# Score tiles of two key tiles shared between VectorE and ScalarE, in a fused attention and gated MLP kernel

## The chip, the cores and the metric

The kernel runs on one core of one Trainium2 chip. Its engines are TensorE (PE; its weight loads are listed apart as PEld), VectorE (DVE), ScalarE (ACT), GpSimd (POOL) and SyncE (SP, which issues nearly all DMAs here). The metric is the device time of one execution in microseconds; lower is better. For a version that was run several times, the median counts.

## The reference

One layer norm feeds an attention of 32 heads and a gated MLP; both results are added to the input. All inputs and the output are bfloat16, with S = 2048 rows, D = 512 columns, heads of 16 columns and F = 1792.

```python
xn = layernorm(A_x)                                   # over the last axis, eps 1e-5
q, k, v = split_heads(xn @ A_wqkv)                    # 32 heads of 16
p = softmax(einsum("bhqd,bhkd->bhqk", q, k) * 16 ** -0.5)
attention = merge_heads(einsum("bhqk,bhkd->bhqd", p, v)) @ A_wo
gate, up = xn @ B_W_gate, xn @ B_W_up
mlp = ((gate * (gate > 0)) * up) @ B_W_down
return A_x + attention + mlp
```

`B_x` is an input that isn't used.

## The kernel before

**Tiling.** The queries are cut into 4 chunks of 512 (`c4`), the heads into 4 groups of 8 (`gg`), each group into its even and odd heads (`ee`), the keys into 16 tiles of 128 (`kt`). One (`c4`, `gg`, `ee`) is a block: 4 heads, 512 queries, 2048 keys. There are 32 blocks, and in each 16 key tiles: 512 combinations that the code calls keys.

For one key there are four score tiles `j` = 0 to 3, one for each head, of 128 keys x 512 queries. PE's array is split into two halves of 64 rows (`half`). A tile `j` uses half `j // 2`; which of the two heads whose columns lie in that half is meant is chosen by `p = j % 2` through the moving operand, a copy of the queries in which all other heads' rows are zero (`qT[..., 2 * p + ee, :]`). The stationary operand, the keys in `kT`, is therefore the same for `j` = 0 and 1, and the same for `j` = 2 and 3.

**Who takes the exponential.** ScalarE takes most keys. It works in units: a unit is one key and one `p`, two score tiles (`j` = `p` and `p + 2`) in two neighbouring PSUM banks, and one activation over 1024 columns turns both into probabilities in `ring` (L1654). There are 704 units; two sets of two banks alternate between them. VectorE takes 160 keys, the quads, all four tiles of each, by an approximation of the exponential in integer arithmetic (`quad`, L1607): one operation a tile from PSUM to `qd` (L1615), then two shifted copies of the four tiles at once, made mostly by POOL (L1629). How many quads a block has is in `QUADS`; where they lie follows from it and from `QUAD_SHIFT`.

**Weighted sums of the values** (PV). `pv_stream` (L1540) makes for each key one group of four matmuls in each half of the array, with the stationary tiles from `v_aug`; a quad has three such groups in each half, for the three patterns.

**Everything else** (projections of queries, keys and values, the MLP's three products, the output projection) is put between the attention's work as jobs. All matmuls of the main part are groups of four, 64 rows x 32 columns, with 512 moving rows, in one half of the array; the tiles that aren't ScalarE's share four PSUM banks (`P_b`), from which VectorE empties them.

**The order.** The program first builds a graph of 8,030 operations. A list written out in the file, `ORDER`, puts all of them in one sequence by their numbers, and each engine's queue is that sequence restricted to the engine. A second list, `SLOTS`, gives the buffer for each tile in turn. Waits on semaphores follow from the graph (`follow`, L543, and `emit`, L579).

**Weight loads.** Each matmul group has a load of its four stationary tiles, and a key that names them (`wkey`). `emit` walks PE's queue and leaves a load out when the half still holds tiles of the same name:

```python
            elif held[o.half] == o.wkey:
                o.load, o.wsrc = False, ()
```

The names are `("k", gg, kt)` for scores and `("v", gg, ee, kt)` for PV. Operations with another name, on the same half, between two of the same name, make a new load necessary.

Of the kernel before, what the change touches and what calls it, by code (L numbers as in the profile page):

```python
# [5 lines left out]
BF16 = mybir.dt.bfloat16  # L6
# [69 lines left out]
SC_ORDER = (0, 2, 1, 3)  # L76
# [11 lines left out]

ORDER = [
# [651 lines left out]
def bass_parallel_sum__mha_block__glu_gated_reglu__prompt_kernel(  # L741
# [13 lines left out]
    with ExitStack() as es:  # L755
# [379 lines left out]
        for bk in blocks:  # L1135
            for t in dve_kt[bk]:
                kinds[bk + (t,)] = KINDS[len(kinds) % len(KINDS)]
# [31 lines left out]
        def first(tile, w, t_w, bank, c, x, need, prio):  # L1169
            for dt in range(DT):  # L1170
# [7 lines left out]
                if dt:  # L1178
                    tile.w.append(o)
# [530 lines left out]
```

## Time and profile before

| | |
|---|---|
| Times of three runs | 677.11, 676.46, 674.73 us; median 676.46 us |
| The profiled execution | span 678.5 us from the first to the last instruction; it is one execution, taken apart from these three runs |
| Granted TensorE clock | 1.000 over the span |
| PE matmuls | 667.7 us busy, 22,348 instructions |
| PE weight loads | 394.5 us busy, 20,912 instructions |
| VectorE | 594.7 us busy, 1,001 instructions |
| ScalarE | 659.1 us busy, 721 instructions |
| GpSimd | 334.1 us busy, 345 instructions |
| DMA | 28.77 MB, 42 GB/s on average |

Busy time is the time in which at least one instruction of the engine was under way. Matmuls are pipelined, and so are ScalarE's activations: two may overlap, so that the pace of an engine is read from the starts of its instructions and not from their durations. A group's line gives the source line, the engine, what is written and read, the shape and the count; then the busy time and the mean duration of one; then the idle time of the engine ahead of it and what ended it. In the timeline a line gives the start and the length of a run of like instructions, with the idle time ahead of it in brackets.

### The profile page before, as it was taken

The numbers are of one execution on the slowest core, as the hardware profiler recorded it, in microseconds if no ns is written. First come the engines' busy times: TensorE is split into PE (matmuls) and PEld (weight loads), VectorE is DVE, ScalarE is ACT, GpSimd is POOL, SyncE is SP. The second block draws the span as 40 slices with busy tenths as digits, with TensorE's granted clock in tenths as the row PEclk, the third lists the DMA queues.
The fourth block names the chain that finished last, engine by engine and source line by source line (L and its number), as shares of the span: only waits on it lengthen the run. The fifth ranks groups of instructions, "written<-read, shape, count | busy, mean of one in ns | idle before, by whom it ended". The sixth has DMA issues, their size and how long they took to land.

```text
span 678.5 us, 46119 instructions
## 1 busy us (share of the span) xinstructions
PE 667.7 (98%) x22348; PEld 394.5 (58%) x20912; DVE 594.7 (88%) x1001; ACT 659.1 (97%) x721; POOL 334.1 (49%) x345
## 2 busy tenths in 40 slices
PE   8999999999999999999999999999999999999997
PEld 3455566565565766665665655555565555555663
DVE  8958999998998888999999787999999777889886
ACT  7999999999999999999999999999999999999995
POOL 3201554654546645555556535654546642535650
PEclk9999999999999999999999999999999999999999
DMA  6420111131411121110101110020200012020101
GB/s 195 58 71 13 43 32 27 24 95 40 118 38 28 37 57 29 27 54 19 38 7 26 36 42 22 23 74 4 59 7 19 22 44 72 23 80 15 31 4 43
DMA packets 51478, 28.77 MB, mean 42 GB/s; under 512 B 18840, under 2 KB 50328, under 8 KB 51288
## 3 DMA queue, kind: packets, MB, share of 16 engines
q1 hardware_dynamic: 51144, 25.70, 14.6%
q8 instruction: 169, 2.77, 1.7%
q14 instruction: 21, 0.17, 0.1%
q10 hardware_dynamic: 144, 0.13, 0.1%
HBM read 18.22 MB, written 2.10 MB: 30 GB/s over the span
## 4 chain that ended last, share of the span: by engine, by line
PE 95%; DVE 2%; ACT 1%; issue 1%; DMA 0%; SPq 0%; POOL 0%
PE ps L481 95%; ACT ring L1654 1%; DVE stats L945 0%; DMA x_sb<-in_A_x_dram 0%; DVE xn_sb L968 0%; SPq L858 0%; DVE xnT L1013 0%; DVE o_sb L1410 0%; DVE up_sb L1412 0%; DVE qf L1414 0%; ACT up_sb L937 0%; DVE o_sb L1407 0%; ACT up_sb L936 0%; POOL rstd L943 0%; ACT xn_sb L1429 0%
## 5 line engine op out<-in xcount | busy, mean ns | idle before, releaser
L1654 ACT ACTIVATE ring<-ps 128x1024 bf16<-128x1024 f32 x704 | 651.1, 1085 | 7.4 <-PE ps L481 6.5
L481 PE MATMUL ps<-qT,kT 64*32 64x512 bf16 x8192 | 470.5, 375 | 1.8 <-issue 0.7
L1615 DVE TENSOR_SCALAR qd<-ps 128x512 int16<-128x512 f32 x640 | 418.8, 685 | 53.4 <-PE ps L481 47.3
L1629 POOL INT64_ADD qd<-qd x312 | 321.0, 1043 | 282.0 <-PE ps L481 132.6
L481 PE MATMUL ps<-qd,v_aug 64*32 64x512 bf16 x3840 | 297.1, 375 | 0.5 <-issue 0.4
L1595 PEld LDWEIGHTS <-kT 64*32 64x32 bf16 x8156 | 178.9, 92 | 113.6 <-issue 26.6
L481 PE MATMUL ps<-ring,v_aug 64*32 64x512 bf16 x2816 | 241.6, 375 | 0.4 <-issue 0.2
L1567 PEld LDWEIGHTS <-v_aug 64*32 64x32 bf16 x5256 | 129.5, 92 | 61.2 <-issue 11.8
L481 PE MATMUL ps<-xnT,wgs 64*32 64x512 bf16 x1792 | 136.7, 375 | 0.6 <-issue 0.6
L481 PE MATMUL ps<-xnT,wus 64*32 64x512 bf16 x1792 | 135.9, 375 | 0.0
L481 PE MATMUL ps<-Wd,hT 64*32 64x512 bf16 x768 | 60.9, 375 | 0.0
L1048 PEld LDWEIGHTS <-wus 64*32 64x32 bf16 x1792 | 45.2, 92 | 22.4 <-issue 2.9
L1048 PEld LDWEIGHTS <-wgs 64*32 64x32 bf16 x1792 | 44.2, 92 | 22.4 <-issue 3.5
L1048 PEld LDWEIGHTS <-hT 64*32 64x32 bf16 x1792 | 44.5, 92 | 21.4 <-issue 2.7
L481 PE MATMUL ps<-Wv,hT 64*32 64x512 bf16 x512 | 44.2, 375 | 0.4 <-issue 0.4
L481 PE MATMUL ps<-Wk,hT 64*32 64x512 bf16 x512 | 43.8, 375 | 0.0
L1269 DVE SCALAR_TENSOR_TENSOR hT<-ps,up_sb 128x512 bf16<-128x512 f32 x56 | 38.5, 687 | 5.5 <-PE ps L481 4.8
L1265 DVE COPY up_sb<-ps 128x512 f32<-128x512 f32 x56 | 38.4, 686 | 3.0 <-PE ps L481 2.1
L481 PE MATMUL ps<-Wo_p,x_sb 64*32 64x512 bf16 x480 | 40.5, 375 | 0.1
L481 PE MATMUL ps<-xnT,Wq 64*32 64x512 bf16 x480 | 36.8, 375 | 0.0
L481 PE MATMUL ps<-xnT,Wk 64*32 64x512 bf16 x480 | 35.6, 375 | 0.9 <-DVE xnT L1013 0.8
L481 PE MATMUL ps<-Wv,xnT 64*32 64x512 bf16 x512 | 31.6, 375 | 0.5 <-DVE kT L1106 0.4
(81 smaller groups left out, 219.6 us busy)
## 6 DMA issues: line engine op xcount, KB each, us to landing
wus<-in_B_W_up_dram SPq DMA_DIRECT2D x38, 128.0 KB, 2.9
wgs<-in_B_W_gate_dram SPq DMA_DIRECT2D x38, 128.0 KB, 2.7
xr_sb<-in_A_x_dram SPq DMA_DIRECT2D x16, 128.0 KB, 2.3
qT<-qf SPq DMA_DIRECT2D x120, 16.0 KB, 2.6
o_sb<-o_sb SPq DMA_DIRECT2D x60, 32.0 KB, 2.4
out_dram<-xn_sb SPq DMA_DIRECT2D x15, 128.0 KB, 2.1
x_sb<-in_A_x_dram SPq DMA_DIRECT2D x8, 128.0 KB, 2.8
Wd<-in_B_W_down_dram SPq DMA_DIRECT2D x6, 128.0 KB, 2.8
```

Of the source, the lines that this page charges most:

```text
L481: return e.add_instruction(mybir.InstMatmult(name=e.bass.get_next_instruction_name(), engine=mybir.EngineType.PE, ins=[e.lower_ap(x), e.lo ...
L1048: e.ldweights(w()[rows, 32 * j:32 * j + 32], tile_position=(rows.start, 32 * j))
L1265: G.op("DVE", 603, lambda e: e.tensor_copy(up_sb[:, tup.slot, :], bank_of(tu)), reads=[tu], writes=[tup], prio=-590)
L1269: G.op("DVE", 603, lambda e: e.scalar_tensor_tensor(out=hT[:, th.slot, :], in0=bank_of(tg), scalar=0.0, in1=up_sb[:, tup.slot, :], op0=ALU ...
L1567: e.ldweights(vs(j), tile_position=(64 * half, 32 * j))
L1595: e.ldweights(ks(m), tile_position=(64 * half, 32 * m))
L1615: G.op("DVE", 601, lambda e, j=j, tx=tx: e.tensor_scalar(qd[:, tq.slot, 512 * j:512 * j + 512], ps[:, BANK[tx.slot], :], IBIAS[3], 0.0, op ...
L1629: G.op("POOL", POOL_NS, lambda e, x=x, n=n: e.int64_add(x().bitcast(I64), raw().bitcast(I64), SHIFTS[n + 1] * LANES), reads=[ti, tq, t_lib ...
L1654: exp_ops[u] = G.op("ACT", ACT_NS, lambda e, tr=tr, k0=k0: e.activation(ring[:, tr.slot, :, :], ps[:, 4 * k0:4 * k0 + 2, :], ACTF.Exp, sca ...
```

## The change

For every quad's key the list `MATES` names a second key tile of the same block, its mate, which belongs to ScalarE. The two exchange half of their tiles. VectorE's four score tiles are now `j` = 0 and 2 of its own key and `j` = 1 and 3 of the mate; ScalarE's two units of the mate are `j` = 0 and 2 of the mate and `j` = 1 and 3 of the quad's key. The quad's scores come in the order 1, 3, 0, 2: the mate's tiles first. The PV groups follow: a group's four stationary tiles are now two of one key tile and two of the other (`kts`), and it needs the values of both. The number of tiles, units, quads and groups on each engine stays what it was; `QUADS`, `QUAD_SHIFT` and the jobs are the same.

`emit` isn't changed: it leaves a load out wherever the half still holds the tiles of that name. `ORDER` and `SLOTS` are replaced as a whole; they hold the same 8,030 numbers and as many slots. A further line puts an ordering edge between the parts of the first projections.

```diff
-SC_ORDER = (0, 2, 1, 3)
+SC_ORDER = (1, 3, 0, 2)
...
+MATES = [[], [0, 8], [1, 3, 4, 6, 8], [1, 2, 4, 6, 9], [1, 2, 4, 6, 9, 12], ...]
...
 ORDER = [
...
 SLOTS = [int(c, 36) for c in (
...
+        mate = {}
+        for n, bk in enumerate(blocks):
+            for t, m in zip(sorted(dve_kt[bk]), MATES[n]):
+                mate[bk + (t,)], mate[bk + (m,)] = m, t
...
                 if dt:
+                    o.order.add(tile.w[-1])
                     tile.w.append(o)
...
-        def pv_stream(key, kt, src, reads, u, prio, src_eng=None):
-            key = part(key + (kt,))
+        def pv_stream(key, kts, src, reads, u, prio, src_eng=None):
+            key = part(key + (kts[0],))
...
-                    return v_flat[rows, kt, a:a + 32]
+                    return v_flat[rows, kts[j % 2], a:a + 32]
...
-                         load=vload, weights=[t_vones, t_v[kt]], wkey=("v", gg, ee, kt))
+                         load=vload, weights=[t_vones, t_v[kts[0]], t_v[kts[1]]], wkey=("v", gg, ee) + kts)
...
         def quad(key, u, prev):
+            other = key[:3] + (mate[key],)
...
             for j in SC_ORDER:
-                prev = score(key, j, tx, ...)
+                prev = score(other if j % 2 else key, j, tx, ...)
...
-                pv_stream(key[:3], key[3], ...)
+                pv_stream(key[:3], (key[3], mate[key]), ...)
...
             for sub in range(2):
-                prev_sc = score(key, p + 2 * sub, ts, ...)
+                prev_sc = score(key if not p else key[:3] + (mate.get(key, key[3]),), p + 2 * sub, ts, ...)
...
-                pv_stream(key[:3], key[3], ...)
+                pv_stream(key[:3], (key[3], mate.get(key, key[3])), ...)
```

More of the change, by code (lines that the diff above doesn't have):

```diff
@@ L87 @@
 QUADS = [0, 2, 5, 5, 6, 6, 4, 5, 6, 5, 5, 5, 6, 5, 5, 8, 5, 5, 4, 6, 6, 4, 6, 5, 5, 5, 5, 5, 5, 6, 5, 5]
+MATES = [[], [0, 8], [1, 3, 4, 6, 8], [1, 2, 4, 6, 9], [1, 2, 4, 6, 9, 12], [1, 2, 6, 9, 12, 15], [2, 5, 7, 12], [0, 2, 5, 6, 9], [1, 2, 3, 7, 10, 13], [0, 4, 8, 10, 12], [1, 2, 5, 6, 9], [1, 2, 4, 6, 8], [1, 2, 4, 6, 7, 12], [1, 3, 6, 8, 11], [1, 2, 4, 6, 9], [1, 3, 5, 7, 9, 13, 15, 11], [8, 10, 12, 14, 15], [5, 9, 11, 14, 15], [3, 6, 9, 11], [1, 2, 4, 7, 9, 14], [1, 2, 5, 9, 12, 15], [2, 5, 7, 10], [1, 2, 4, 6, 9, 12], [1, 4, 6, 9, 14], [1, 4, 6, 9, 11], [1, 2, 4, 5, 8], [1, 2, 4, 5, 8], [1, 2, 4, 5, 8], [0, 2, 4, 6, 10], [1, 2, 4, 7, 10, 14], [1, 2, 5, 9, 11], [1, 2, 3, 6, 11]]
@@ L427 @@
-    "934032106200317200212130290021e30f0421350020011200c0123401d00a1b420208012009617001123113103e11001f031203134130151010310c16d301431a1b01821291"
-    "026117210202112301e231f1021140015013401010001131c0032d14ab01830911376702130100110123")]
+    "000121133020010120122113230401510617000008193210a101b220c01330de1f3100110145203120210103a12b031013890617200c1d1001e30f1230016110741520003111"
+    "0a31b120811209c321d20e1f1130232130302167130011131830a01b21021453001cd230101899001613074120301231001a11ef0031100ab30120101001c23011d031030440"
@@ new lines @@
+    "1b3000516710020e1010f01331890002c321300103111240a2103210b601017200c301330dd01ef320134205800120320409021233e0210020401620173210a23311f203bc01"
+    "d304003145320008121020902101100301103670e11g022113f123201a113110b411513060134133207831101243009c11h1d30e21f320a320110b3014530002321331i40013"
+    "10103000167140300113890133j1ab1001ef1030c210321d1003101020331106730040114301052101200103189001001a1210bc2114120de131f00211123032001261020742"
+    "215020010111200a01210012031b1240211cd08121933030223131030111ef22011ab2410c201310d61731304003145220030512301811930013312302010212670c02163120"
@@ new lines @@
+    "0d11ef0001a014212002b01000020711893122041312010561137200211300120a1b40310020100181013019301ef300167300040013cd00331ab23100421024050011122002"
+    "103230821110209101ef200021cd00232410ab0206317200132102145100003010343001e01f3001233100c1331d0018930300124011ab301416701113022011124510220110"
+    "2203e1141f21101cd210189233001012230131ab300611322074015303021e02012f000218000922110311301011100041c110210d420102315002621700a011020b22112341"
+    "250381419300211011020c3210003d43013005603317012200e2114020f213ab00218012009c4301d2302013305001245132000121014001612130307c11d3300016a1b32023"
@@ new lines @@
+    "102e30f11189147302112310340123206501167080211013230c31241300de22113120f01a13109020b811193001012341000103141005631310c307c11d0010402101001a03"
+    "1b010d31ef0124101230010101673433040001503022011314891003110130c1213g10da0312300be3121f03082241113030719123h0312630742152000101200e322401020f"
+    "a201b212080121009c100d60312030743105031230030e001f3000231100413101a1301b0189231016017201400123c110d421510020131112000112220136212107a21041b1"
+    "201018920301ef20302112003310c300d6010213003703114204015320331ef11003301ab130803100130931230430010131201c011d0060123011210074315130101ef4320a"
@@ new lines @@
+    "102403112011b80192011023113403c311220d021140101e21001f02163171510341315020a3101b20008021130922313227031421450020101220cd031ef920a01230b60032"
+    "1307a1011204302042133120c0311200de111fb220143012530813219301a031b1024302313233061700023e0011120130e1110f102f11cd30401512032114893061111g3000"
+    "72312320331a232030b010h001e21f00021420114530i20132cd0832190206301207200j13012003e310003f02401032011014501210a1102130bc1d02210123101010204216"
+    "70230181020130129e10400fa232210002b310210131cd21034201305821934302331672023120203a1320b1cd3103e1f0014303100141011210520131111001318009c12101"
@@ new lines @@
+    "1000de24101f0011601207a32011b001000014015010108940c0120d6011230700143123230120a3320be231f203003110012145210140c31100d23311126702313231100a23"
+    "141020b01110230001891200112ef041153001203101cd1300123300430167010010112001a1511106013b01ef0332304131003571890030101cd3400001103120211a0380b2"
+    "113013021301360007e03139013f1400158330111309c11d32021132103311ab04113311670031311108120100942100205e2340120fc001d20200121ab00021110011e23241"
+    "0f23123033412350820193062311342020711012cd30201ab01061010200418902130014570001111023")]
@@ L1574, in pv @@
                     return ins
-                o = G.op("PE", 216, pv, reads=[t_vones, t_v[kt]] + reads, joins=[t], prio=prio, name="pv%d" % u, mode="half", half=half, bank=(t, 0), slack=PV_SLACK if src_eng is None else PAT_SLACK,
-                         load=vload, weights=[t_vones, t_v[kt]], wkey=("v", gg, ee, kt))
+                o = G.op("PE", 216, pv, reads=[t_vones, t_v[kts[0]], t_v[kts[1]]] + reads, joins=[t], prio=prio, name="pv%d" % u, mode="half", half=half, bank=(t, 0), slack=PV_SLACK if src_eng is None else PAT_SLACK,
+                         load=vload, weights=[t_vones, t_v[kts[0]], t_v[kts[1]]], wkey=("v", gg, ee) + kts)
                 pv_ops[key].append(o)
@@ L1613, in quad @@
                 tx = Tile("x", P_b, XBANKS)
-                prev = score(key, j, tx, lambda tx=tx: BANK[tx.slot], 0, u, u - 1000, [prev] if prev else [], 1, after=u - AHEAD)
+                prev = score(other if j % 2 else key, j, tx, lambda tx=tx: BANK[tx.slot], 0, u, u - 1000, [prev] if prev else [], 1, after=u - AHEAD)
                 G.op("DVE", 601, lambda e, j=j, tx=tx: e.tensor_scalar(
@@ L1634, in quad @@
             for t, x, more in ((ti, raw, [tq]), (ta, xa, []), (tb, xb, [])):
-                pv_stream(key[:3], key[3], [(lambda rows, j=j, x=x: x()[rows, 512 * j:512 * j + 512].bitcast(BF16)) for j in range(4)],
+                pv_stream(key[:3], (key[3], mate[key]), [(lambda rows, j=j, x=x: x()[rows, 512 * j:512 * j + 512].bitcast(BF16)) for j in range(4)],
                           [t] + more, u, u + PV_LAG, "DVE")
@@ L1651, in bass_parallel_sum__mha_block__glu_gated_reglu__prompt_kernel @@
             for sub in range(2):
-                prev_sc = score(key, p + 2 * sub, ts, lambda b=4 * k0 + sub: b, sub, u, u - 2000 + 0.1 * sub, [prev_sc] if prev_sc else [], 2, pair=u)
+                prev_sc = score(key if not p else key[:3] + (mate.get(key, key[3]),), p + 2 * sub, ts, lambda b=4 * k0 + sub: b, sub, u, u - 2000 + 0.1 * sub, [prev_sc] if prev_sc else [], 2, pair=u)
             tr = Tile("r%d" % u, P_ring)
@@ L1658, in bass_parallel_sum__mha_block__glu_gated_reglu__prompt_kernel @@
                 trs = [where[key + (i,)] for i in range(2)]
-                pv_stream(key[:3], key[3], [(lambda rows, j=j, trs=trs: ring[rows, trs[j % 2].slot, j // 2, :]) for j in range(4)], trs, u, u + PV_LAG)
+                pv_stream(key[:3], (key[3], mate.get(key, key[3])), [(lambda rows, j=j, trs=trs: ring[rows, trs[j % 2].slot, j // 2, :]) for j in range(4)], trs, u, u + PV_LAG)
             while made_q < len(quads) and (quads[made_q][0] <= u + AHEAD or u == NU - 1):
```

20 lines of the change are left out of this document (removed), and 630 rows, old and new, of the table ORDER.

## The prediction

> **What bounds the kernel now.** I read the page first: the busy times, then the costliest groups and the DMA queues.
>
> ```profile
> span 678.5 us, 46119 instructions
> PE 667.7 (98%) x22348; PEld 394.5 (58%) x20912; DVE 594.7 (88%) x1001; ACT 659.1 (97%) x721; POOL 334.1 (49%) x345
> PE 95%; DVE 2%; ACT 1%; issue 1%; DMA 0%; SPq 0%; POOL 0%
> L1654 ACT ACTIVATE ring<-ps 128x1024 bf16<-128x1024 f32 x704 | 651.1, 1085 | 7.4 <-PE ps L481 6.5
> L1615 DVE TENSOR_SCALAR qd<-ps 128x512 int16<-128x512 f32 x640 | 418.8, 685 | 53.4 <-PE ps L481 47.3
> L1595 PEld LDWEIGHTS <-kT 64*32 64x32 bf16 x8156 | 178.9, 92 | 113.6 <-issue 26.6
> L1567 PEld LDWEIGHTS <-v_aug 64*32 64x32 bf16 x5256 | 129.5, 92 | 61.2 <-issue 11.8
> q8 instruction: 169, 2.77, 1.7%
> ```
>
> PE and ACT both look full, and the chain of waits gives PE 95%. Two full engines can't both be the limit, so I went to the timeline of ScalarE alone, and looked at when its exponentials (L1654) start.
>
> ```profile
> 10.48 1.96 ACT L1654 ACTIVATE ring<-ps 128x1024 bf16<-128x1024 f32 x2
> ...
> 47.22 12.02 ACT L1654 ACTIVATE ring<-ps 128x1024 bf16<-128x1024 f32 x13
> ...
> 58.07 2.08 ACT L1654 ACTIVATE ring<-ps 128x1024 bf16<-128x1024 f32 x2
> ...
> 392.25 3.77 ACT L1654 ACTIVATE ring<-ps 128x1024 bf16<-128x1024 f32 x4 [0.17 <-PE ps L481]
> 396.67 7.49 ACT L1654 ACTIVATE ring<-ps 128x1024 bf16<-128x1024 f32 x8 [0.65 <-PE ps L481]
> ...
> 610.07 58.88 ACT L1654 ACTIVATE ring<-ps 128x1024 bf16<-128x1024 f32 x64 [0.29 <-PE ps L481]
> 669.43 0.66 ACT L1405 ACTIVATE up_sb<-ps 128x256 f32<-128x256 f32 x2 [0.48 <-PE ps L481]
> ```
>
> From 47.22 to 58.07 us twelve starts follow one another: 10.85 / 12 = 0.904 us from one exponential to the next, which is the pace of an undisturbed ScalarE (one takes 1.085, so they overlap). The 704 of them run from 10.48 to 610.07 + 58.88 = 668.95 us, 658.5 us. At the undisturbed pace they would take 703 x 0.904 + 1.08 = 636.6. So ScalarE is the limit, it does the same 704 exponentials after the change, and all that can be won between them is 658.5 - 636.6 = **22 us**. The page's idle time shows 7.4 of it; the rest is lateness that fits into the overlap of two exponentials and makes no gap.
>
> Each exponential waits for PE's scores. So the next question is why PE is late, and the timeline of PE around the larger gaps of ScalarE answers it.
>
> ```profile
> 394.98 0.38 PE L481 MATMUL ps<-Wd,hT 64*32 64x512 bf16 x4
> 395.10 0.38 PE L481 MATMUL ps<-qd,v_aug 64*32 64x512 bf16 x4
> 396.02 0.39 PE L481 MATMUL ps<-qT,kT 64*32 64x512 bf16 x4 [0.55 <-ACT ring L1654]
> 396.24 0.39 PE L481 MATMUL ps<-Wd,hT 64*32 64x512 bf16 x4
> 396.24 0.10 PEld L1048 LDWEIGHTS <-hT 64*32 64x32 bf16 x4
> 396.25 0.38 PE L481 MATMUL ps<-qT,kT 64*32 64x512 bf16 x4
> 396.45 0.39 PE L481 MATMUL ps<-Wd,hT 64*32 64x512 bf16 x4
> ...
> 562.50 2.85 ACT L1654 ACTIVATE ring<-ps 128x1024 bf16<-128x1024 f32 x3
> 564.65 0.38 PE L481 MATMUL ps<-Wv,hT 64*32 64x512 bf16 x2
> 565.40 0.38 PE L481 MATMUL ps<-Wv,hT 64*32 64x512 bf16 x2 [0.37 <-issue]
> 566.03 7.61 ACT L1654 ACTIVATE ring<-ps 128x1024 bf16<-128x1024 f32 x8 [0.68 <-PE ps L481]
> ...
> 591.25 2.88 ACT L1654 ACTIVATE ring<-ps 128x1024 bf16<-128x1024 f32 x3
> 592.57 0.38 PE L481 MATMUL ps<-xnT,wgs 64*32 64x512 bf16 x2
> 593.52 0.37 PE L481 MATMUL ps<-xnT,wgs 64*32 64x512 bf16 x2 [0.58 <-issue]
> 594.64 15.14 ACT L1654 ACTIVATE ring<-ps 128x1024 bf16<-128x1024 f32 x16 [0.51 <-PE ps L481]
> ```
>
> At 564.65 and at 592.57 PE stops in the middle of a group of four matmuls that share one wait: two start, then nothing for 0.75 and 0.95 us, then the other two. They need no new weights and no semaphore. What is missing is the instruction itself. Numbering PE's and PEld's records in order of start, I find 32 such stops (over 0.22 us without a start, and the next record carries no wait) between these two:
>
> ```profile
> 46.98 0.12 PEld L1048 LDWEIGHTS <-xnT 64*32 64x32 bf16 x11 [0.18 <-issue]
> ...
> 609.43 0.09 PEld L1567 LDWEIGHTS <-v_aug 64*32 64x32 bf16 x1 [0.57 <-issue]
> ```
>
> All 32 stand at a record number that leaves the same rest when divided by 256. The q8 row fits: 169 pieces for 22,348 + 20,912 = 43,260 PE instructions, 256 in each, and 2.77 MB / 43,260 = 64 bytes for one. Its share gives 0.017 x 16 x 678.5 / 169 = 1.1 us per piece. So **PE's instruction supply** runs dry at the seam of two pieces. The stops add up to 11.6 us (each counted beyond 0.06 us); 24 of them lie in 364 to 427 and 552 to 608 us.
>
> What a stop costs ScalarE: 392.25 + 4 x 0.904 = 395.87, and the next exponential came at 396.67, 0.80 late after a stop of 0.92 (395.10 to 396.02); by the same reckoning 0.82 late after 0.75 and 0.68 after 0.95. That is 2.30 for 2.62, 0.88. So the stops cost 11.6 x 0.88 = **10.2 us** of the 22.
>
> **The change part by part.** *Work that stays.* 704 exponentials, 640 evacuations on VectorE (L1615), the same matmuls, POOL additions and DMAs: VectorE's four tiles are only two heads each of two key tiles instead of four of one. Cost 0. Two dependencies are new: a quad needs keys and values of its mate too. For 91 of 160 quads the mate is the neighbouring key tile, and both lie in the same block; I price that at 0, with the keys' projection, due 32 units ahead, as its cover. Without the cover one quad would wait for at most a projection's place in the queue, and VectorE sits idle 53.4 us before these evacuations already.
>
> *Fewer weight loads.* A load is left out when the half of the array already holds that stationary tile. Counted in the order lists: before, 9 of 2,048 score groups and 350 of 1,664 PV groups go without, which gives (2048 - 9) x 4 = 8,156 and (1664 - 350) x 4 = 5,256 loads, just the counts of the two PEld rows. After, it is 355 and 618. That is 614 groups, 2,456 loads fewer, 5.7% of PE's instructions: 40,804, or 159 pieces.
>
> Price of the load itself: at 396.24 the next group's load (0.10) runs under a group that started at 396.24, and that half's next group starts at 396.45, 0.21 later, the time the moving rows take. A load so hidden gives back nothing: 0. What it gives back is room for the fetch. At ScalarE's pace, 256 instructions are 256 / (43,260 / 704) x 0.904 = 3.77 us of PE's work before and 256 / (40,804 / 704) x 0.904 = 3.99 us after. Each piece so gets 0.22 us more; taking 0.23 off every one of the 32 stops leaves 4.5 of 11.6 us. Gain 7.1 x 0.88 = **-6.2 us**. The ends: 0, if the loads are left out elsewhere than where the supply is short, and -10.2, if no stop is left, which neighbouring pieces make possible since relief is handed on.
>
> [...]
>
> *Order and score order (1, 3, 0, 2).* All queues are reordered, SP's and POOL's too; the first exponentials and the tail wait for the same work, 0. What I can read off the lists is how evenly PE serves ScalarE. Between the score pair of one unit and the next, the fuller half holds 4 groups in 440 gaps before, 5 in 203, 6 or more in 3; after, 4 in 247, 5 in 306, 6 in 57, 7 or more in 8. Over two gaps in a row 10 or more stand in 6 places before and in 98 after (88 with 10, 9 with 11, one with 12). A group takes 0.215 us (396.02 to 396.24 to 396.45). Two exponentials take 1.81. A score group can't start before the exponential two units back has ended (1.085), and its result starts the next 0.42 later (396.25 to 396.67), so 1.81 - 1.085 - 0.42 = 0.30 us is to spare. Ten groups, 2.15, are 0.04 over 1.81 + 0.30, eleven 0.255, twelve 0.47: 88 x 0.04 + 9 x 0.255 + 0.47 = 6.3 us, against 0.9 before. One heavy gap belongs to two such pairs, so I take half: **+2.7 us**. The ends: 0, and +25.6 when nothing is to spare (57 x 0.385 + 7 x 0.60 + 0.81 less 1.4 before).
>
> The remaining lateness, 22 - 10.2 = 11.8 us, comes from waits for banks and for VectorE, whose order is new as well. Nothing quoted says which way it moves: 0, with ends of half of it, -6 and +6.
>
> Sum: -6.2 + 2.7 = -3.5 us. Against the profiled execution (678.5 us, 2.0 above the median of the runs) that is 675.0; carried to the median of 676.46, **673.0 us**. About 0.3%, 2 us, is what a measurement of this kernel can tell from no change.
>
> **The rivals.** *All stops go and the order is better too.* For it: the supply is short by 0.36 us a stop on average, little more than a piece gains. Against it: the gaps counted above. -10.2, with up to half of the other 11.8: 660 to 668 us. 0.10.
>
> *The two effects cancel.* The relief is spread evenly, not where the 24 stops are, and the gaps cost the full 5.4: within 2 us of 676.5. 0.16.
>
> *The bunched order starves ScalarE: slower.* The place is the score pair behind six or more groups of its half. With half of the 0.30 already used up, as after any other wait, 57 x 0.235 + 7 x 0.45 + 0.66 = 17 us, less 0.9 before, +16 against -6.2: 686 us. It decides as soon as these 65 gaps cost more than 0.1 us each. For it: 65 against 3 is much, and 53.4 us of VectorE's waiting shows how little PE has in reserve. Against it: a light gap behind a heavy one pays some back. 0.27.
>
> *The saved instructions are worth nothing.* The stops stay, because a piece's own latency of 1.1 us and more sets them, not the number of instructions. Then 676.5 + 2.7 = 679.2 us. Against it: the common rest by 256. 0.05. [...]
>
> **How the numbers follow.** The forecast, 668 to 674.4, has 0.42. Faster by over 0.3%: 0.42 + 0.10 = 0.52; the same: 0.16; slower: 0.27 + 0.05 = 0.32. The range goes from 664, half of the best rival, to 686, the price of the bunched order; about one in ten lies on either side.
>
> **What would show it.** Right: PEld with about 18,456 instructions (kT 6,772, v_aug 4,184), q8 with 159 or 160 pieces, stops at seams few and below 5 us in sum, ScalarE's exponentials still 0.904 apart at best and their whole run 3 to 4 us shorter. Wrong: ScalarE's idle time before L1654 above 7.4 us with PE as releaser and no seam near; or as many seam stops as before with fewer instructions between them; or a VectorE that waits for PE much longer than 47.3 us, with the loss in the waits that I set at 0.

## The result, and the profile after

The changed kernel takes 711.55 us (median of 4 runs, 710.4 to 712.4) against 676.79 us for the kernel before on the same chip: 1.0507 times as long, 95% interval 1.0481 to 1.0532. It is **slower by 35 us**; the prediction had said 673.0, with 686 as its upper end. The profiled execution took 712.4 us.

The page of the kernel after, in the lines that answer to those of before:

```profile
span 710.6 us, 43731 instructions
PE 693.5 (98%) x22348; PEld 353.6 (50%) x18456; DVE 597.4 (84%) x1001; ACT 673.2 (95%) x721; POOL 335.6 (47%) x345
q8 instruction: 160, 2.62, 1.6%
PE 86%; DVE 4%; SPq 4%; DMA 2%; issue 2%; ACT 1%; POOL 1%; DVEq 0%; POOLq 0%
L1663 ACT ACTIVATE ring<-ps 128x1024 bf16<-128x1024 f32 x704 | 665.2, 1031 | 20.3 <-PE ps L484 15.0
L1624 DVE TENSOR_SCALAR qd<-ps 128x512 int16<-128x512 f32 x640 | 418.1, 685 | 62.9 <-PE ps L484 56.0
L1603 PEld LDWEIGHTS <-kT 64*32 64x32 bf16 x6772 | 146.0, 92 | 123.7 <-issue 37.2
L1575 PEld LDWEIGHTS <-v_aug 64*32 64x32 bf16 x4184 | 100.4, 92 | 74.7 <-issue 26.7
```

The loads are what the lists said: 6,772 and 4,184, 18,456 in all. VectorE's operations and their durations are the same. What grew is ScalarE's idle time ahead of its exponentials (L1663; 7.4 before, 20.3 now), with PE as releaser, and VectorE's wait for PE (47.3 before, 56.0 now). Both engines get their scores later. The timeline of ScalarE alone, its first and its last row of exponentials:

```profile
15.73 5.78 ACT L1663 ACTIVATE ring<-ps 128x1024 bf16<-128x1024 f32 x6 [0.71 <-PE ps L484]
...
663.38 37.18 ACT L1663 ACTIVATE ring<-ps 128x1024 bf16<-128x1024 f32 x39 [0.20 <-PE ps L484]
```

The 704 exponentials run from 15.73 to 663.38 + 37.18 = 700.56 us, 684.8 us; before it was 658.5, from 10.48 on. So 26.4 us are lost between exponentials and 5.2 ahead of the first, 31.6 of the 35 us; most of the rest is that the profiled execution of the kernel before was a long one (its span of 678.5 us lies above its median time of 676.5, and in the other runs the span is about 2 us shorter than the time). In what follows the **lateness** of a kernel is the sum, over its exponentials, of what the time from one start to the next exceeds 0.9045 us, ScalarE's own pace: 21.5 us before, 47.9 after.

Numbered as in the prediction (PE's sequencer records, 128 before, have to be counted too), PE's records now show **no stop** at a seam of its instruction pieces: 32 with 11.6 us before, 0 after. Whether the saved loads took them away or the slower pace did, a run below decides; in either case a much larger loss lies on top.

### The profile page after: what moved, and what is told of

Its sections match the earlier page's. It is cut to its first block, busy times and chain, and to the rows that moved or that the text cites. A ratio compares the mean times of both kernels' runs of the same rounds, so it can differ in the third digit from the quotient of the medians.

```text
span 710.6 us, 43731 instructions
## 1 busy us (share of the span) xinstructions
PE 693.5 (98%) x22348; PEld 353.6 (50%) x18456; DVE 597.4 (84%) x1001; ACT 673.2 (95%) x721; POOL 335.6 (47%) x345
## 4 chain that ended last, share of the span: by engine, by line
PE 86%; DVE 4%; SPq 4%; DMA 2%; issue 2%; ACT 1%; POOL 1%; DVEq 0%; POOLq 0%
PE ps L484 85%; DVE qd L1624 2%; ACT ring L1663 1%; SPq L1099 1%; DMA Wq<-in_A_wqkv_dram 1%; SPq L1260 1%; DMA o_sb<-o_sb 1%; SPq L1518 1%; PE ps L1181 0%; SPq L861 0%; POOL qd L1638 0%; SPq L1527 0%; DVE stats L948 0%; DVE hT L1277 0%; DMA rb<-rrec 0%
## 5 line engine op out<-in xcount | busy, mean ns | idle before, releaser
L1663 ACT ACTIVATE ring<-ps 128x1024 bf16<-128x1024 f32 x704 | 665.2, 1031 | 20.3 <-PE ps L484 15.0
L484 PE MATMUL ps<-qT,kT 64*32 64x512 bf16 x8192 | 486.2, 375 | 4.4 <-DVE qd L1624 2.4
L484 PE MATMUL ps<-qd,v_aug 64*32 64x512 bf16 x3840 | 262.5, 375 | 0.1
L484 PE MATMUL ps<-ring,v_aug 64*32 64x512 bf16 x2816 | 231.7, 375 | 0.6 <-DVE qd L1624 0.2
L1603 PEld LDWEIGHTS <-kT 64*32 64x32 bf16 x6772 | 146.0, 92 | 123.7 <-issue 37.2
L1575 PEld LDWEIGHTS <-v_aug 64*32 64x32 bf16 x4184 | 100.4, 92 | 74.7 <-issue 26.7
L484 PE MATMUL ps<-xnT,wgs 64*32 64x512 bf16 x1792 | 134.6, 375 | 0.4 <-PE ps L484 0.2
L484 PE MATMUL ps<-Wd,hT 64*32 64x512 bf16 x768 | 64.6, 375 | 0.1
L1051 PEld LDWEIGHTS <-wus 64*32 64x32 bf16 x1792 | 43.1, 91 | 35.5 <-issue 10.9
L484 PE MATMUL ps<-Wk,hT 64*32 64x512 bf16 x512 | 45.8, 375 | 0.0
```

The source lines that it names most:

```text
L484: return e.add_instruction(mybir.InstMatmult(name=e.bass.get_next_instruction_name(), engine=mybir.EngineType.PE, ins=[e.lower_ap(x), e.lo ...
L1051: e.ldweights(w()[rows, 32 * j:32 * j + 32], tile_position=(rows.start, 32 * j))
L1575: e.ldweights(vs(j), tile_position=(64 * half, 32 * j))
L1603: e.ldweights(ks(m), tile_position=(64 * half, 32 * m))
L1663: exp_ops[u] = G.op("ACT", ACT_NS, lambda e, tr=tr, k0=k0: e.activation(ring[:, tr.slot, :, :], ps[:, 4 * k0:4 * k0 + 2, :], ACTF.Exp, sca ...
```

## The experiments

The file has two separable parts: the new tiles (`MATES` and what follows from it) and the new `ORDER`, `SLOTS` and `SC_ORDER`. All ratios are to the kernel before, timed beside each kernel on the same chip; since the kernel before took 676.8 to 680.8 us on them, kernels timed on different chips are compared by ratio. Lateness and first exponential are read from one profiled execution of each kernel, which can lie a few us off its median: that of before lies about 3.5 us above, that of mates_old_order 2.2 below. Line numbers move where the list has more lines (L1663 becomes L1683).

| Kernel | Median us | Ratio, 95% interval | Lateness us | First exponential us |
|---|---|---|---|---|
| before | 676.79 | 1 | 21.5 | 10.48 |
| after | 711.55 | 1.0507 [1.0481, 1.0532] | 47.9 | 15.73 |
| mates_old_order | 676.58 | 0.999 [0.9963, 1.0017] | 15.8 | 10.29 |
| new_order_no_mates | 709.28 | 1.0491 [1.0469, 1.0513] | 45.9 | 14.77 |
| after_all_loads | 713.07 | 1.0543 [1.0524, 1.0563] | 48.6 | 15.02 |
| before_all_loads | 691.62 | 1.0191 [1.0142, 1.024] | 37.1 | 10.24 |
| after_first_loads | 708.15 | 1.0447 [1.0418, 1.0475] | 49.0 | 10.70 |
| after_interleaved | 695.73 | 1.0271 [1.0237, 1.0306] | 30.3 | 15.62 |
| before_uninterleaved | 710.55 | 1.0486 [1.0456, 1.0515] | 51.5 | 10.24 |
| after_interleaved_2 | 693.72 | 1.0183 [1.0133, 1.0233] | 32.6 | 12.52 |
| after_waits_later | 690.99 | 1.019 [1.0149, 1.0232] | 30.2 | 10.62 |
| after_alternated | 693.47 | 1.022 [1.0185, 1.0255] | 33.1 | 10.49 |
| after_evened | 688.75 | 1.0103 [1.0069, 1.0137] | 26.9 | 10.53 |
| mates_evened | 688.21 | 1.0154 [1.0127, 1.018] | 29.9 | 10.32 |
| mates_even_pess | 686.09 | 1.008 [1.0054, 1.0106] | 26.5 | 10.38 |
| mates_even_cal | 681.30 | 1.0015 [0.9982, 1.0048] | 23.2 | 10.33 |
| mates_waits_pe | 680.91 | 1.0033 [1.0005, 1.0061] | 20.9 | 10.52 |
| mates_waits_all | 682.94 | 1.0078 [1.0053, 1.0103] | 24.8 | 10.25 |
| mates_alternated | 680.63 | 1.0013 [0.9986, 1.0041] | 21.7 | 10.31 |
| mates_alternated_2 | 680.51 | 1.002 [0.9992, 1.0048] | 18.2 | 10.26 |

**The two parts apart.** mates_old_order has the new tiles in the old order, new_order_no_mates the old tiles in the new order:

```diff
 # mates_old_order: after, with before's lists
-SC_ORDER = (1, 3, 0, 2)
+SC_ORDER = (0, 2, 1, 3)
 ORDER = [
...
 # new_order_no_mates: before, with after's lists
-SC_ORDER = (0, 2, 1, 3)
+SC_ORDER = (1, 3, 0, 2)
 ORDER = [
...
```

> The tiles are shared between quad and mate as after the change, but all queues stand in the order of before, with the quad's scores in the old order 0, 2, 1, 3 (71 score groups and 350 PV groups go without a load, against 9 and 350). Theory order: the new order alone costs the time, and sharing tiles is free; 676 us, between 672 and 680, exponentials' idle time as before (7.4 us), first exponential near 10.5 us. Theory mates: sharing is what delays (PV groups need two key tiles, quads need the mate's keys); 695 to 712 us.

> The new order of all queues and the new score order 1, 3, 0, 2, with four tiles of one key tile for VectorE as before (62 score groups and 618 PV groups without a load). Theory order: 705 to 715 us, first exponential near 15.7 us, 35 to 50 us of lateness of the exponentials. Theory mates: 676 to 685 us.

Sharing the tiles costs nothing (0.999) and the new order alone costs nearly all (1.0491 of 1.0507). The quad's score order went with the lists in both kernels; it wasn't tried by itself. The old order with the new tiles, on its page:

```profile
L1663 ACT ACTIVATE ring<-ps 128x1024 bf16<-128x1024 f32 x704 | 649.3, 1093 | 3.4 <-PE ps L484 2.9
L1624 DVE TENSOR_SCALAR qd<-ps 128x512 int16<-128x512 f32 x640 | 418.5, 685 | 47.9 <-PE ps L484 41.9
q8 instruction: 168, 2.75, 1.8%
```

**The price of the loads.** Both kernels with every load made:

```diff
-            elif held[o.half] == o.wkey:
+            elif False:
```

> The changed kernel with every stationary tile loaded again, 973 groups or 3,892 loads more. Theory order: the queues' order sets the time, loads are hidden, and PE is slow enough that 256 instructions last 3.9 us: 711 to 717 us with few seam stops. Rival, loads left out do harm (a group without its own load is bound to the one before it): 690 to 705 us. Rival, the instruction supply is what the change lives on: seam stops come back as before, 10 us and more, 720 to 725 us.

> The kernel before with every stationary tile loaded again, 359 groups or 1,436 loads more; order and tiles unchanged. Theory supply: 44,696 PE instructions, a piece of 256 lasts 3.65 us instead of 3.77, so every seam stop grows by 0.12 us and more seams stop: 15 to 25 us of stops instead of 11.6, 680 to 689 us. Rival, the supply is worth nothing to the time: 675 to 678 us.

In the old order 1,436 loads more make it 1.0191 times as long; at 691.62 us, 690 by the ratio, it is above the theory's 680 to 689, so a load costs more there than was reckoned. The page shows where:

```profile
q8 instruction: 175, 2.87, 1.7%
L1654 ACT ACTIVATE ring<-ps 128x1024 bf16<-128x1024 f32 x704 | 656.6, 1057 | 17.4 <-PE ps L481 15.5
```

Its trace has 64 stops at the seams with 28.8 us, 17.2 more than before, and 15.7 us more lateness, 0.91 us for each us of stops (the profiled execution took 696.1 us, 4.5 above the median, so these two numbers are somewhat large). So instruction supply does limit the old order, and the price of 0.88 fits. In the new order 3,892 loads more change 1.0507 to 1.0543, with 8 stops and 2.3 us: there the loads are worth little either way, and nearly all stops are gone even with every load made. The reading that fits both, the author's own and not measured by itself: in the new order PE, late for other reasons, gives the supply the time that it needs for the next 256 instructions (28.8 us of stops in the old order and 2.3 in the new, with every load made in both). **The loads saved and the order's loss don't add up; the loss swallows the gain.**

**The head.** In the kernel after, the first query tile waits, as the timeline of its first microseconds shows:

```profile
11.92 1.90 PE L1181 MATMUL ps<-xnT,Wq 128*32 128x384 bf16 x32 [3.83 <-DMA Wq<-in_A_wqkv_dram]
...
13.45 1.57 ACT L1207 ACTIVATE qT<-ps,hmask 128x384 bf16<-128x384 f32 x4 [4.72 <-PE ps L1181]
```

The view of the tile Wq gives when its first DMA was issued, and how long its two DMAs took to land, in the kernel after and (second fence) before:

```profile
L874 SPq DMA_DIRECT2D Wq<-in_A_wqkv_dram x1: 516/516/516, 5.1 to 5.1; - x1
DMA to landing us min/median/max: 6.1/6.4/6.8
```

```profile
L871 SPq DMA_DIRECT2D Wq<-in_A_wqkv_dram x1: 434/434/434, 2.6 to 2.6; - x1
DMA to landing us min/median/max: 2.6/5.4/8.1
```

The first DMA is the one with 6.8 us in the kernel after and with 2.6 before: it was issued 2.5 us later, just behind two transfers of 512 KB (Wv at 4.09 and hT at 4.57 us; before, only four of 128 KB stood ahead of it), and took 4.1 us longer to land.

after_first_loads puts SyncE's first 16 DMAs back in the program's order; nothing else is moved:

```diff
 # SyncE's queue, first 16 entries of ORDER (23 is the first part of Wq)
-19, 20, 21, 22, 25, 24, 26, 29, 32, 23, 27, 33, 28, 30, 34, 31
+19, 20, 21, 22, 23, 24, 25, 26, 27, 28, 29, 30, 31, 32, 33, 34
```

> The kernel after with one edit: the first 16 DMAs of SyncE's queue (x, Wq, Wk, Wv) are issued in the order of the program, so the first part of Wq is fifth again instead of tenth. Theory: the first query tile waited 4.7 us for TensorE, which waited 3.8 us for this DMA; the first exponential starts at 11 to 12 us instead of 15.7 and the time falls by 4 to 5 us, to 706.5 to 708 us, with the lateness of the later exponentials as after (46 to 49 us). Rival (the head's later start is made by the order of TensorE's first groups, or is caught up later): 710 to 712.5 us.

```profile
10.70 5.69 ACT L1683 ACTIVATE ring<-ps 128x1024 bf16<-128x1024 f32 x6
```

The first exponential starts 5.0 us earlier and the time falls by 3.4 us (by the ratios 0.0060, 4.1 us), somewhat less than the 4 to 5 expected. The rest of the lateness is where it was: 49.0.

**How the halves stand in PE's queue.** In the new order groups of one half stand in longer rows: 176 rows of four or more against 34. after_interleaved moves groups only past groups of the other half; before_uninterleaved does the opposite to the old order. In both, each half's own sequence and its loads, and the queues of ScalarE, VectorE, GpSimd and SyncE, are unchanged. The edit to `ORDER` is of the kind (h0, h1: the halves):

```diff
 # PE's queue around unit 346, after (-) and after_alternated (+)
-score 346 h0, MLP h0, MLP h0, MLP h0, score 346 h1
+score 346 h0, PV h1, MLP h0, score 346 h1, MLP h0, quad score h1, MLP h0
```

> The kernel after with one edit: in TensorE's queue, groups of one half are moved ahead of or behind groups of the other half (by at most a dozen entries at a time). Each half keeps its own sequence of groups and so its loads (973 groups without loads, as after), and the queues of ScalarE, VectorE, GpSimd and SyncE stay as they are. Theory (completions in queue order): a score pair is signalled only when the older groups of the other half are done, and a wait holds back everything queued behind it on both halves; taking out the places where a score pair stands behind a long run of the other half takes off 12 to 18 us: 693 to 700 us, the lateness of the exponentials falls from 47.9 to 30-36 us, and pairs signalled over 0.52 us after their last start fall from 72 of 704 to under 40. Rival (bunching within each half: too many groups fall into one gap between exponentials; or banks that are held too long): the sequences of the halves and of all other engines are unchanged, so 709 to 713 us.

> The kernel before with one edit: groups of TensorE's queue are moved at random by at most a dozen entries past groups of the other half only, until runs of four or more groups of one half are 120 (34 before, 176 after). Each half's sequence, the loads and all other queues stay as before. Theory (completions in queue order and waits that hold both halves): slower by 10 to 28 us, 687 to 705 us. Rival (the new order's loss comes from what falls into a gap on each half, or from banks): 674 to 679 us.

Both went the way of the theory: 15.8 us gained, and 33 us lost, 5 more than the top of that range, by nothing but the order of the two halves against each other. One figure missed: the pairs signalled over 0.52 us after their last start fell from 72 to 50 only, where under 40 were expected.

**What the order of the halves does** is seen at unit 346. The timeline of PE in the kernel after, then that of ScalarE:

```profile
352.11 0.58 PE L484 MATMUL ps<-qT,kT 64*32 64x512 bf16 x8
352.32 0.38 PE L484 MATMUL ps<-xnT,wgs 64*32 64x512 bf16 x4
352.52 0.38 PE L484 MATMUL ps<-qT,kT 64*32 64x512 bf16 x4
352.54 0.38 PE L484 MATMUL ps<-xnT,wgs 64*32 64x512 bf16 x4
352.74 0.38 PE L484 MATMUL ps<-ring,v_aug 64*32 64x512 bf16 x4
352.75 0.38 PE L484 MATMUL ps<-xnT,wgs 64*32 64x512 bf16 x4
```

```profile
349.10 3.83 ACT L1663 ACTIVATE ring<-ps 128x1024 bf16<-128x1024 f32 x4 [0.16 <-PE ps L484]
353.22 1.94 ACT L1663 ACTIVATE ring<-ps 128x1024 bf16<-128x1024 f32 x2 [0.29 <-PE ps L484]
```

The row at 352.11 holds two groups: unit 346 on half 0, and at 352.31 its other group on half 1. The three MLP groups on half 0 (`wgs`) stand between them in the queue, and all three start after the second score group. Yet the exponential starts at 353.22: 0.91 after that group, but 0.47 after the last of the three older MLP groups (352.75). It was due 0.9045 after the fourth of the row at 349.10 (351.91), at 352.81, so 0.41 are lost. In after_alternated the same groups start at the same distances:

```profile
339.08 0.38 PE L504 MATMUL ps<-qT,kT 64*32 64x512 bf16 x4
339.09 0.38 PE L504 MATMUL ps<-qd,v_aug 64*32 64x512 bf16 x4
339.30 0.38 PE L504 MATMUL ps<-xnT,wgs 64*32 64x512 bf16 x4
339.31 0.38 PE L504 MATMUL ps<-qT,kT 64*32 64x512 bf16 x4
339.51 0.38 PE L504 MATMUL ps<-xnT,wgs 64*32 64x512 bf16 x4
339.52 0.38 PE L504 MATMUL ps<-qT,kT 64*32 64x512 bf16 x4
339.73 0.38 PE L504 MATMUL ps<-xnT,wgs 64*32 64x512 bf16 x4
```

```profile
336.11 6.64 ACT L1683 ACTIVATE ring<-ps 128x1024 bf16<-128x1024 f32 x7 [0.29 <-PE ps L504]
```

There unit 346 is the fifth of these seven and starts at 339.79, 0.48 after its second group (339.31), with no gap ahead of it. **Here a score pair is signalled only when all groups that are older in the queue are done, those of the other half too.** Over all units of the kernel after, 65 score pairs had overtaken an older group by more than 0.1 us; they are signalled 0.53 to 1.15 us after their own last start (median 0.635), and 0.42 to 0.50 us after the last start of an older group (median 0.436, as it is for all pairs after their own start). With 14 pairs that overtook by less, the delays add up to 15.3 us; before there were 10 pairs over 0.1 us, 17 in all, with 1.8 us.

The other half of the loss is a **wait at the head of the queue**. Sorting the lateness of the kernel after by what the last score group of each unit did when it should have started: 17.0 us are signals later than the usual 0.44 us after it, 26.6 us lie behind groups on its own half, and 4.2 us pass while a waiting group of another kind stands ahead in the queue. Of the 26.6, 22.8 us are in backlogs that begin with a group of another kind that had to wait for a bank, VectorE, GpSimd or ScalarE. Before, the first two were 6.3 and 10.5 us, and the backlogs of that kind 6.6. Such a wait holds both halves: in the kernels before and after, 2,419 and 2,516 groups wait for another engine or the other half, and in their traces no group of either half that stands behind one of them started ahead of its release. Many of these waits are PE's for itself: a group waits when the group ahead of it in its bank was in the other half (`follow`). In the kernel after 335 groups other than score pairs started within 80 ns of a release by the other half and 304 of one by VectorE; before, 238 and 273.

**The second attempt, and the waits.** Three more kernels try to get the rest out of PE's queue, all with the first DMAs mended: after_interleaved_2 shortens rows further, after_waits_later also queues groups a little behind the time at which their inputs are there (this one changes the order within the halves, and 184 loads come back), after_alternated lets the halves take turns nearly everywhere (676 groups follow one of their own half, 2,294 in after). after_evened moves the queues of VectorE, GpSimd and SyncE too.

> The kernel after with the first 16 DMAs in the program's order (worth 3.4 us before) and the two halves interleaved once more in TensorE's queue only, now sparing long runs: after_interleaved showed the other half's next group held 209 ns behind 32 instructions of one half and 231 behind 40, against 10 to 18 ns behind 4 to 16. Theory (queue order between the halves makes most of the loss): lateness of the exponentials falls from 30 us in after_interleaved to 20-26 us, time 682 to 688 us. Rival (what after_interleaved left is made by the order within each half and on the other engines): 690 to 694 us, the 695.7 of after_interleaved less the head alone.

> The kernel after with the first 16 DMAs in the program's order and all queues moved on from after_interleaved in small steps, loads about as few as after (899 groups without). Theory: with few loads no stops, and with short runs lateness of 12-18 us: 669 to 677 us. Rival (few loads want groups of the same keys near each other, which costs what they save): 680 to 690 us.

> The kernel after with two edits: the first 16 DMAs in the program's order (worth 3.4 us before), and TensorE's queue alone put in another order, in which a group is queued some 0.1 to 0.2 us behind the time at which its input or its bank is there, so that few groups wait at the queue's head; 184 of the 973 groups without loads get their loads back. The queues of ScalarE, VectorE and GpSimd are as in after. Theory (waits of other groups at the head of TensorE's queue pile up a backlog in which the score groups stand: 22.8 of the 47.8 us in after; and completions in queue order: 17.0 us): lateness falls from 48 to 16-26 us, 676 to 688 us. Rival (the other engines' new order is what costs): above 692 us, like after_interleaved_2 (693.7).

> The kernel after with two edits: the first 16 DMAs in the program's order (worth 3.4 us before), and TensorE's queue merged anew from the two halves' own sequences so that the halves alternate nearly everywhere: a group follows one of its own half 676 times (2,294 in after, 2,123 in after_interleaved_2, 1,722 in the old order). Sequences and loads of each half and all other queues are as in after. Theory A (what costs is that one half's groups stand in line before the other half's): well below after_interleaved_2, 678 to 687 us, lateness 18 to 25 us. Theory B (what is left in after_interleaved_2 comes from the order within the halves and on the other engines): 690 to 698 us.

after_alternated came out as the rival said, and so did after_interleaved_2 in microseconds; on its chip the kernel before took 680.8 us, and by its ratio, 689 us, it lies between the two theories, as after_waits_later does. Its late first exponential, 12.52 in the table, came in an execution in which the first rows of x arrived 0.7 us later than in after_first_loads and the granted clock of the first 20 us was 0.91. after_evened missed the range of the theory and ended with the rival. Three quite different queues for PE end within 1.0183 to 1.022. after_alternated has nearly no overtaking left (8 pairs, 1.8 us), and after_interleaved_2 still 46 pairs with 10.0 us, at the same time. By the sorting above, from after the late signals fell by 10.2 us in after_alternated and 7.4 in after_interleaved_2, the backlogs by 5.8 and 7.8. So **what the halves' order in the queue costs is 15 to 18 us** (1.0447 less 1.022 and less 1.0183, each uncertain by 3 to 4 us by the intervals); how it divides between signals and backlogs depends on the queue.

**The same rules on the old order.**

> The new score tiles in the old order (676.6 us), with an order moved on from it in small steps by the rules read from the traces: a score pair does not stand behind a run of the other half, a group whose input is late does not stand ahead of others, and the pieces of 256 TensorE instructions are spread evenly; the loads stay about the same (about 420 groups without). Theory: the lateness of 15.8 us falls to 8-12 us, 668 to 674 us. Rival (the lateness left over is made by what these rules do not hold): 675 to 685 us.

> The new score tiles in the old order (676.6 us), moved on in small steps on all queues as mates_evened was, but with runs of four or more groups of one half kept at 48 (34 in the old order, 111 in mates_evened). Theory (mates_evened lost 11 us by its long runs): lateness 11 to 16 us, 671 to 677 us. Rival (the losses come from the other moves): 683 to 690 us as mates_evened.

> As mates_even_pess, but moved on further, with 58 runs of four or more groups of one half. Theory: lateness 9 to 16 us, 668 to 677 us; rival: 683 to 690 us.

> The new score tiles in the old order (676.6 us), with TensorE's queue alone put in another order by the same rule; 411 groups without loads (421). Theory: the lateness of 15.8 us, half of it in backlogs that begin with a wait, falls to 10-14 us: 669 to 675 us. Rival (what is left has other causes, or such small moves cost by themselves as in mates_evened and mates_even_cal): 678 to 688 us.

> As mates_waits_pe, with small moves on the queues of VectorE, GpSimd and SyncE as well. Theory: 668 to 675 us. Rival: 678 to 688 us.

> The new score tiles in the old order with TensorE's queue merged anew from the halves' own sequences so that they alternate: a group follows one of its own half 376 times (1,722 in the old order). All else as in mates_old_order (676.6 us, lateness 15.8 us). Theory A (each same-half neighbour costs): lateness 9 to 13 us, 669 to 674 us. Theory B (alternation by itself is worth nothing where the old order has its waits and banks in step): 676 to 682 us.

> As mates_alternated, with small moves within the halves as well so that groups are queued a little behind their inputs (266 same-half neighbours, 411 groups without loads against 421). Theory A: 667 to 674 us. Theory B (moves within the halves cost, as in mates_waits_pe, 680.9 us): 678 to 686 us.

None gained. mates_evened lost 11 us against the old order, above both of its ranges; it has 111 long rows, but these aren't shown to be the cause: with 48 rows it was 1.008 and with 58 only 1.0015. By the ratios (682 and 678 us) these two lie between their ranges. The four others came out as their rivals said, and none of the seven went below the old order. The kernel with the best ratio stays mates_old_order, and its interval holds 1: no version was found that beats the kernel before.

mates_alternated is useful for another reason. In it, as in after_alternated, the halves take turns, so what is left between the two, 1.022 less 1.0013, 14.0 us, is hardly the halves' order against each other. Their pages:

```profile
L1683 ACT ACTIVATE ring<-ps 128x1024 bf16<-128x1024 f32 x704 | 658.7, 1037 | 11.3 <-PE ps L504 8.2
```

```profile
L1683 ACT ACTIVATE ring<-ps 128x1024 bf16<-128x1024 f32 x704 | 651.8, 1066 | 6.9 <-PE ps L504 5.9
```

The first is after_alternated. Counted within each half's own sequence from one unit's score group to the next, the fuller half has at most 4 groups in 323 gaps, 5 in 335 and 6 or more in 45; in the old order 501, 199 and 3. A group takes 0.2155 us and an exponential 0.9045, so five already are 0.17 over. Measured, a gap of at most 4 costs 23 ns of lateness in after_alternated and 16 in mates_alternated, a gap of 5 costs 62 and 64, a gap of 6 or more 109 in the first. With 16, 64 and 109 the first kernel's gaps come to 5.2 + 21.4 + 4.9 = 31.5 us and the second's, at its own three prices, to 21.7: 9.8 of the 11.4 us between them. But these prices hold stops of the instruction supply: mates_alternated has 22 stops at the seams with 8.6 us, after_alternated, which makes fewer loads and is slower, one with 0.6. The 43 gaps of mates_alternated in which a stop lies, or up to 1.2 us behind one, carry 7.6 of its 21.7 us. Without such gaps a gap of at most 4 costs 11 ns there and one of 5 costs 43, against 22 and 62 in after_alternated; the two kernels then lie some 18 us apart, and the larger number of full gaps makes about 8 of them at 11, 43 and 109. So bunching explains less than half; the rest is that each gap costs more, and no run shows why. Nor was the bunching isolated, for the two kernels also differ in the queues of the other engines and in the loads.

**The sum.** From after to mates_old_order, by the ratios: the first DMAs 4.1 us, the halves' order against each other 15.4 (to after_alternated), what is in the halves' sequences and the other engines 14.0, and 1.6 from mates_alternated to mates_old_order, within the intervals. Together 35.0; as differences along one chain they must add up, so the sum is no check on the causes. The 14.0 are what is left after the saved loads have taken the stops away.

## Why the prediction was wrong

**What bounds the kernel: right.** ScalarE waits for PE's scores, and the seams cost about what was said: 0.88 predicted, 0.91 in before_all_loads, from one execution of each kernel. The rival that instructions are worth nothing is refuted by the same run: 1,436 loads more, 1.0191 times the time.

**Work that stays, at 0: right.** mates_old_order shows that tiles of two keys are free.

**Fewer loads, -6.2 us: the mechanism right, the sum wrong.** 18,456 loads, 160 pieces and stops below 5 us were all as listed under what would show it, though the last sign tested nothing: with every load made the new order has only 2.3 us of stops. But the term was added to the order's, and it can't be: in the new order the loads are worth 0.0036, 2.4 us, with overlapping intervals. The old order with the new tiles shows the other side: 62 groups' loads fewer and 20 stops with 6.1 us in place of 32 with 11.6, and in the profiled executions 5.7 us less lateness; the medians of the runs show no gain, and these two executions lie as far apart by their distance from their medians, so the 5.7 us are not shown to be the loads'.

**Order and score order, +2.7 us: the step that failed.** It has three faults.
- The price began at ten groups in two gaps. It begins at five in one gap, with 62 ns against 23 for at most four in after_alternated, and the new order has 136 more gaps of five. Bunching so comes to 8 to 10 us where +2.7 were put down.
- It counted groups on each half as if the halves had nothing to do with each other. They share one queue, and signals and waits pass through it in order: 15 to 18 us by after_alternated and after_interleaved_2, of which the prediction had nothing.
- "The first exponentials and the tail wait for the same work, 0": the same work, but its DMA stood tenth in place of fifth in SyncE's queue, 4.1 us. Each queue past which a step moves had to be looked at, and the numbers were in the list.

**The remaining lateness at 0 (-6 to +6)** assumed that waits for banks and VectorE stay alike. The backlogs that begin with such a wait went from 6.6 to 22.8 us (part of the same microseconds, sorted another way).

**The rivals.** The bunched order that starves ScalarE had the right sign and 0.27; its threshold, 0.1 us for each of the 65 heavy gaps, was passed: counted by places in the queue, as the prediction does, they cost 187 ns each in the kernel after, 12.1 us of its 47.9. By the halves' own sequences there are only 45 heavy gaps, with 6.3 us, and the 335 gaps of five carry 29.0. So it named the right place for part of the loss only; the 306 gaps of five by its own count, with 24.9 us, it took for free unless two stood in a row. What would have shown the forecast wrong, ScalarE's idle time above 7.4 us with PE as releaser and no seam near, is just what came.

**Open:** how much of the last 14 us is bunching within the halves, how much the order of VectorE and GpSimd, and why each gap costs more in the new order; no kernel here took the bunching away and left the rest (after_waits_later, with 54 fewer gaps of five but 13 more of six and over, gained 2 us on after_alternated by the ratios, within the intervals).

## What to carry to other kernels

When two halves of the array are fed from one queue, count each half's work, but also what stands between two groups that an engine needs together: here the 65 score pairs that had overtaken an older group of the other half by more than 0.1 us were signalled 0.42 to 0.50 us after the last older start, and none of the 2,516 waits in the kernel after was passed by a younger group of either half. A gain at one limit (instruction supply) can't simply be added to a loss at another; here, while the second held, the first was worth 0.0036, 2.4 us. Where a list reorders every queue, look at the first entries of the DMA queue by name: one weight that stood five places later cost 4.1 us here (after_first_loads).

## What was not expected of the hardware

- Signals in queue order across the halves, with starts out of it: medians 0.436 us after the last older start against 0.635 after the own, for 65 pairs.
- Behind a row of one half the other half's next group, waiting for nothing, is late by 12 to 25 ns after 8 or 16 instructions, and by about 0.15 us after 32, in the kernel after. In the rows of 32 some group always waits; behind rows in which none waits (up to 24 instructions) it is late by 2 ns at most. So the length of a row isn't shown to be what costs.
- In the kernel after, PE waited 3.8 us at the head and the granted clock of the first 20 us was 0.83; in the kernel before it was 1.00. The 32 matmuls behind that wait (11.92) took 1.90 us, against 1.20 in the kernel before and 1.26 in after_first_loads, which have no such wait:

```profile
0.00:20.00 20.00, 13.81 (x178) 6.24 (x166) 12.63 (x46) 11.06 (x19) 5.38 (x16) 0.83 0.64 185
```

```profile
0.00:20.00 20.00, 16.23 (x266) 7.11 (x270) 17.20 (x57) 15.21 (x23) 7.53 (x20) 1.00 0.56 166
```

The columns are the window, then the busy time and the instructions of PE, PEld, DVE, ACT and POOL, the granted clock, the DMA share and GB/s.
